# Windowed attention and a gated feed-forward block in one kernel: where the first gate's and the first value's products stand on TensorE

## The chip, the cores and the metric

The kernel runs on one core of a Trainium2 chip. The metric is the device time of one execution in microseconds (us), lower is better.

## What is computed

Attention over 8 batches, 8 heads, 576 positions and 64 features a head, with a causal window of 64 positions, followed by a gated feed-forward block over the 4608 tokens (512 features, 1536 hidden). Cut to what matters:

```python
scores = scale * np.matmul(q, k.transpose(0, 1, 3, 2))
mask = (rel >= 0) & (rel < 64)          # rel = query position - key position
scores = np.where(mask, scores, -1e9)
attn = softmax(scores)
x = np.matmul(attn, v)                  # heads side by side: (4608, 512)
gate = 1.0 / (1.0 + np.exp(-(x @ w_gate)))
val = x @ w_val
out = (gate * val) @ w_out
```

The three weights arrive as float64 and are turned into float32 on the chip.

## The kernel before, in words

Tokens are worked on in 12 tiles of 384. Attention is cut into units: a unit (t, p) is tile t and one pair of heads p, p from 0 to 3. The program has three stages. The front computes the attention of tiles 0 and 1, eight units in a row. The second stage runs the feed-forward block of tiles 0 and 1 with plain products, while the weights are still being converted and tile 2 and 3's attention is slipped in. The rest takes two tiles at a time with seven combined products in place of eight, and the next tiles' attention between them.

A unit of the front passes through all engines:

- `scores` (line 220, tile `s`): 24 small matmuls on TensorE, into two banks of the accumulation memory (PSUM), one for each half h.
- `exponentials`: VectorE adds the mask, scales and takes the row minimum (line 244, tiles `p` and `mn`), three instructions a half; ScalarE takes the exponentials (line 252), three a half. For the first half it also sums them.
- `normalize`: VectorE sums the second half (line 265), corrects and inverts the sums (lines 259 and 260, tile `rs`), GpSimd multiplies (line 269).
- `stage_b`: TensorE transposes the two halves (line 301, tile `pp`), ScalarE copies them out (line 306, tile `pT`).
- `stage_c`: 24 small matmuls give the unit's attention output (line 331, tile `oo`). `x_split` turns it into a high part, which ScalarE rounds off (line 338), and a low part, which VectorE gets by subtraction (line 339): tile `x`.

In the feed-forward block `up` (line 362, tile `ph`) makes one 128 x 384 piece of the hidden layer with 12 matmuls: for each of the four head pairs high weight times high x, high weight times low x, low weight times high x. `up_gate` does this with the gate's weight and takes the sigmoid on ScalarE (line 371, tile `g`). `up_val` does it with the value's weight and multiplies by the gate on VectorE (line 395). `down` adds the piece to the outputs (line 409, tile `y`). The weights are converted by ScalarE (lines 117 and 118), VectorE (lines 126 to 130), ScalarE again (line 158) and VectorE (line 159), each kind shortly before its use, with DMAs of the converted weights to memory (line 154) in the queue of SyncE.

What sets the order: every step is put into a list with a time and a rank, the list is sorted by both, and the steps are written in that order. TensorE keeps the written order (`keep_in_program_order`). The other engines are ordered by a scheduler, with one rule that matters here: exponentials and sigmoids need different function tables in ScalarE, so all of them form one chain in written order (`table_order`, with `chain`), and a table load stands wherever the chain goes from one kind to the other. All engines execute their instructions in order.

The times of the front are written out by hand. Unit n (0 to 7) has its scores at -40 + 3.6n and its softmax 3.5 later. So the softmax of unit (1,2), n = 6, has the time -14.9 (in floating point -14.899999999999999), the scores of unit (1,3) have -14.8 and its softmax has -11.3. The first gate, `up_gate` of tile 0 and piece 0, is at -9.9 and the first value at -7.8.

The banks for the `ph` tiles go round among three; the first gate's was last used by the scores of unit (1,1).

Of the kernel before, what the change touches and what calls it, by code (L numbers as in the profile page):

```python
# [26 lines left out]
def attn_ffn(ctx: ExitStack, tc: tile.TileContext, qT, kT, vN, w_gate, w_val, w_out, out, outT):  # L27
# [57 lines left out]
    def pe(ins):  # L85
        return tc.keep_in_program_order(ins)
# [262 lines left out]
    def h_bank(nm):  # L349
        nbank[0] += 1  # L350
        return psum(0, nbank[0] % 3, nm)[:, :TT]

    def up(t, j, m):
        ph = h_bank(f"ph{m}_{t}_{j}")
        w2 = wgv[m][j]
        prs = []
        for p in range(NP):
            whi, wlo = (w2[:, p // 2, e, p % 2 * P:(p % 2 + 1) * P] for e in range(2))
            xh, xl = xs[(t, p)][:, 0, :], xs[(t, p)][:, 1, :]
            prs += [(whi, xh), (whi, xl), (wlo, xh)]  # L360
        for i, (l, r) in enumerate(prs):
            pe(nc.tensor.matmul(ph, l, r, start=i == 0, stop=i == len(prs) - 1))  # L362
        return ph
# [12 lines left out]
    def up_gate(t, j):  # L376
        gate_table(t, j, up(t, j, 0))
# [13 lines left out]
    def up_val(t, j):  # L391
        ph = up(t, j, 1)
        g = gates.pop((t, j))
        h32 = mp.tile([P, TT], F32, name=f"h32_{t}_{j}", tag="c", bufs=CB)
        nc.vector.tensor_mul(out=h32, in0=ph, in1=g)
        last = hidden_split(t, j, h32, nc.vector)
        if t == 0:
            marks[j] = (chain[-1], last.ins)
# [103 lines left out]
    def sums_make(m, k):  # L502

        a1, a2 = sums[m, k]
        sw = mp.tile([P, 4, H], F32, name=f"sw_{m}_{k}", tag="raw", bufs=RAW)
        lo, up = ([slice(h + c, h + c + P) for c in range(0, H, P)] for h in (0, H))
        for c, d in zip(lo, up):
            nc.gpsimd.tensor_add(out=sw[:, 0, c], in0=a2[:, c], in1=a2[:, d])
        for c in lo:
            nc.gpsimd.tensor_sub(out=sw[:, 1, c], in0=sw[:, 0, c], in1=a1[:, c])  # L510
        for c in lo:
            nc.gpsimd.tensor_sub(out=sw[:, 2, c], in0=a1[:, c], in1=a2[:, c])
        for c, d in zip(lo, up):
            nc.gpsimd.tensor_sub(out=sw[:, 3, c], in0=a1[:, d], in1=sw[:, 1, c])
        sums[m, k] = sw
# [189 lines left out]
    UPT, DNT, PRT = 4.2, 2.1, 1.05  # L705
    events = []

    def put(tm, o, f, *a):
        events.append((tm, o, f, a))
# [16 lines left out]
    for n in range(2 * NP):  # L726
        t, p = divmod(n, NP)
# [17 lines left out]
    at, now = {}, 0.0  # L745
# [5 lines left out]
    def attend(i):  # L751
        nonlocal now
        for f, t, p, *done in fill.get(i, ()):
            if f in (0, 3):
                put(now - LOAD_AHEAD, 8, load_qk, t, p)
                put(now - LOAD_AHEAD, 8.5, load_v, t, p)
            put(now, 6, stages[f], t, p, *done)
            now += APT[f]

    for i, (kind, t, j) in enumerate(plan):  # L760
        attend(i)
        at[(kind, t, j)] = now
        if (kind, t, j) == ("up", 0, 0):
            now = -9.9
        if kind == "up":
            put(now, 9, up_gate, t, j)
            now += UPT / 2
            attend(i + 0.5)
            put(now, 9, up_val, t, j)
            now += UPT / 2  # L770
        else:
            for x in range(TB):
                put(now + x * DPT, 9, down, t, j, x, j == 0, j == NF - 1)
            now += DNT
        if (kind, t, j) == ("up", 0, 0):
            now = 0.0
    for i in range(KINDS * NF):
        j, m = divmod(i, KINDS)
# [125 lines left out]
    for tm, _, f, a in events:  # L904
        if f in (conv_a, conv_b, conv_c):
            with ExitStack() as behind:
# [4 lines left out]
                j, m = divmod(a[0], KINDS)  # L911
# [56 lines left out]
```

## Time and profile before

| | |
|---|---|
| median of 3 runs | 961.45 us (961.2 to 963.39) |
| profiled execution | 961.67 us, of which the span from first to last instruction is 959.9 us |
| TensorE busy | 941.3 us (98%) |
| TensorE weight loads busy | 898.0 us (94%) |
| VectorE, ScalarE, GpSimd busy | 714.3, 602.7, 147.5 us |
| granted TensorE clock, mean over the span | 0.998 |

PE is TensorE, PEld its weight loads, DVE is VectorE, ACT ScalarE, POOL GpSimd, SP SyncE. Rows of the timeline give the start in us from the span's start, the length, engine, line, operation, output<-input, size, the number of merged instructions, and in brackets the idle time before the row with what ended it. Rows of the windows give, for each stretch, its length and the busy time of every engine, the granted TensorE clock as a fraction of full speed (PEclk), the DMA share and the GB/s.

### The profile page before, as it was taken

Reading aid. Unit: us, or ns where it says so; the run is one execution under the profiler, and the core shown is the slowest. Engines: PE = TensorE matmul, PEld = TensorE weight load, DVE = VectorE, ACT = ScalarE, POOL = GpSimd, SP = SyncE. Lnnn points to the kernel's source line nnn. Section 1 sums busy time; section 2 is a strip of 40 time slices with the busy share of each in tenths; the row PEclk is TensorE's granted clock in tenths of the full one; section 3 lists DMA queues with packets and bytes.
Section 4 is the critical chain, followed back from the end, with each engine's and each line's share of the span. In section 5 each row is a group of like instructions: output and inputs, shape, how many; then the busy total and the mean of one; then the engine's idle time right before and its main releaser. Section 6 shows DMA issues by size and latency. Waiting matters only on the chain.

```text
span 959.9 us, 20420 instructions
## 1 busy us (share of the span) xinstructions
PE 941.3 (98%) x7164; PEld 898.0 (94%) x7164; DVE 714.3 (74%) x1919; ACT 602.7 (63%) x1487; POOL 147.5 (15%) x232
## 2 busy tenths in 40 slices
PE   6899999999999999999999999999999999999998
PEld 5799998879998999999999999999999999999998
DVE  7898989788778985666976576796566697567782
ACT  7878878667677754766755666764666675222350
POOL 4210103703765000110100111100110100000000
PEclk9999999999999999999999999999999999999999
DMA  9899988979988999888889888879988868988464
GB/s 339 304 357 370 347 303 271 347 275 358 369 301 271 402 325 309 277 265 269 251 260 316 267 273 261 270 256 284 302 273 249 268 220 257 314 249 251 143 217 157
DMA packets 105510, 273.45 MB, mean 285 GB/s; under 512 B 11456, under 2 KB 33600, under 8 KB 105408
## 3 DMA queue, kind: packets, MB, share of 16 engines
q1 hardware_dynamic: 105408, 272.15, 84.7%
q8 instruction: 57, 0.93, 0.4%
q14 instruction: 45, 0.37, 0.1%
HBM read 220.20 MB, written 51.90 MB: 283 GB/s over the span
## 4 chain that ended last, share of the span: by engine, by line
PE 77%; ACT 6%; DVE 5%; DMA 5%; issue 3%; POOL 2%; SPq 0%; DVEq 0%; ACTq 0%; POOLq 0%
PE pr L586 42%; PE y L586 23%; PE s L220 3%; PE pp L301 2%; PE ph L362 2%; PE y L409 2%; DMA w32d<-w 2%; PE s L331 2%; ACT p L252 2%; DMA a<-w32d 1%; PE oo L331 1%; DVE w L130 1%; POOL ws L528 1%; ACT L252 1%; ACT raw L118 1%
## 5 line engine op out<-in xcount | busy, mean ns | idle before, releaser
L586 PE MATMUL pr<-x_T,wt 128*128 128x384 f32 x1224 | 227.5, 338 | 0.0
L586 PE MATMUL y<-h,wot 128*128 128x384 f32 x1260 | 219.9, 334 | 0.0
L586 PEld LDWEIGHTS y<-h,wot 128*128 128x128 f32 x1260 | 218.2, 188 | 0.6 <-DVE h L629 0.3
L586 PEld LDWEIGHTS pr<-x_T,wt 128*128 128x128 f32 x1224 | 211.6, 188 | 4.5 <-issue 3.6
L586 PE MATMUL pr<-x_B,wt 128*128 128x384 f32 x1008 | 189.4, 336 | 0.0
L586 PEld LDWEIGHTS pr<-x_B,wt 128*128 128x128 f32 x1008 | 174.7, 188 | 0.8 <-issue 0.5
L668 ACT CAST h<-h 128x384 fp32r<-128x384 f32 x210 | 102.7, 515 | 80.6 <-PE y L586 43.3
L269 POOL TENSOR_TENSOR p<-p,rs 128x384 f32<-128x384 f32 x76 | 66.4, 890 | 551.8 <-DVE rs L260 496.7
L669 DVE TENSOR_TENSOR h<-h,h 128x384 fp32r<-128x384 f32 x210 | 110.7, 554 | 26.8 <-ACT h L668 26.1
L252 ACT ACTIVATE p<-p,mn 128x128 f32<-128x128 f32 x288 | 110.9, 393 | 10.2 <-DVE mn L244 9.7
L362 PE MATMUL ph<-x,w 128*128 128x384 f32 x576 | 107.0, 339 | 1.3 <-ACT g L371 0.8
L362 PEld LDWEIGHTS ph<-x,w 128*128 128x128 f32 x576 | 99.5, 188 | 4.3 <-ACT g L371 1.4
L371 ACT ACTIVATE g<-c 128x384 f32<-128x384 f32 x90 | 46.6, 524 | 66.3 <-DVE c L625 65.9
L244 DVE CUSTOM_DVE_ANT_0 p<-s,m 128x128 f32<-128x128 f32 x288 | 65.3, 284 | 27.6 <-PE s L220 27.5
L629 DVE TENSOR_TENSOR h<-c,g 128x384 f32<-128x384 f32 x90 | 55.5, 616 | 30.2 <-ACT g L371 24.7
L371 ACT ACT_TABLE_LOAD x40 | 51.3, 1283 | 12.7 <-DVE c L625 11.4
L220 PE MATMUL s<-k,q 64*64 64x128 f32 x1152 | 46.5, 293 | 7.2 <-DMA k<-in_kT_dram 5.8
L596 DVE TENSOR_TENSOR c<-pr,p 128x384 f32<-128x384 f32 x60 | 33.0, 550 | 23.7 <-PE pr L586 23.7
L252 ACT ACT_TABLE_LOAD x39 | 50.0, 1283 | 0.7
L252 ACT ACTIVATION_READ_ACCUMULATOR p<-p,mn 128x1 f32 x264 | 49.8, 188 | 0.0
L220 PEld LDWEIGHTS s<-k,q 64*64 64x64 f32 x1152 | 34.2, 141 | 13.9 <-DMA q<-in_qT_dram 5.2
L301 PE MATMUL pp<-ident,p 128*128 128x128 f32 x288 | 42.6, 281 | 4.6 <-POOL p L269 2.6
(106 smaller groups left out, 1215.9 us busy)
## 6 DMA issues: line engine op xcount, KB each, us to landing
wt<-wd SPq DMA_DIRECT2D x186, 512.0 KB, 4.5
wot<-wod SPq DMA_DIRECT2D x105, 512.0 KB, 4.7
v<-in_vN_dram SPq DMA_DIRECT2D x48, 384.0 KB, 5.4
wd<-ws SPq DMA_DIRECT2D x48, 256.0 KB, 4.4
k<-in_kT_dram SPq DMA_DIRECT2D x48, 224.0 KB, 5.2
q<-in_qT_dram SPq DMA_DIRECT2D x48, 192.0 KB, 5.1
w32d<-w SPq DMA_DIRECT2D x36, 256.0 KB, 4.6
wd<-w SPq DMA_DIRECT2D x36, 256.0 KB, 5.8
```

The costliest lines, as they stand in the source:

```text
L220: pe(nc.tensor.matmul(sc[h][half * BLK:(half + 1) * BLK, u, :], qt[h * BLK:(h + 1) * BLK, U * BLK:(U + 1) * BLK], kt[h * BLK:(h + 1) * BLK ...
L244: nc.vector.tensor_tensor_reduce(out=pt[:, u, :], in0=sc[:, u, :], in1=masks[key], op0=ALU.add, op1=ALU.min, scale=-SCALE, scalar=3.0e38, ...
L252: exp = nc.scalar.activation(pt[:, u, :], pt[:, u, :], AF.Exp, bias=mn[:, u:u + 1], scale=-1.0, **sums)
L269: eng.tensor_mul(out=pt, in0=pt, in1=rs.unsqueeze(2).broadcast_to([P, UP, P]))
L301: pe(nc.tensor.transpose(pp[:, u, :], pt[:, u, :], ident))
L362: pe(nc.tensor.matmul(ph, l, r, start=i == 0, stop=i == len(prs) - 1))
L371: act = nc.scalar.activation(g, c, AF.Sigmoid)
L586: pe(nc.tensor.matmul(ps, l, r, start=first and i == 0, stop=last and i == 2, skip_group_check=not check))
L596: marks["plus"] = nc.vector.tensor_add(out=o, in0=ps, in1=a).ins
L629: nc.vector.tensor_mul(out=hidden(s, k)[2 * r + b], in0=c, in1=gates.pop((t, j)))
L668: nc.scalar.copy(h2[:, 0, :], src)
L669: nc.vector.tensor_sub(out=h2[:, 1, :], in0=src, in1=h2[:, 0, :].bitcast(F32))
```

## The change

The first gate's time becomes -14.9, and the first value's -9.9, the time that the gate had. In `up`, the first gate alone (tile 0, piece 0; the value too, since both go through the same function) takes the matmul with the low part of the last head pair's x at the very end of its twelve.

```diff
@@ up
             prs += [(whi, xh), (whi, xl), (wlo, xh)]
+        if t == 0 and j == 0:
+            prs.append(prs.pop(-2))
         for i, (l, r) in enumerate(prs):
@@ the plan
         if (kind, t, j) == ("up", 0, 0):
-            now = -9.9
+            now = -9.9 - UPT / 2
         if kind == "up":
-            put(now, 9, up_gate, t, j)
+            put(now if t + j else -14.9, 9, up_gate, t, j)
             now += UPT / 2
             attend(i + 0.5)
             put(now, 9, up_val, t, j)
```

`UPT / 2` is 2.1. Lines behind the change are two higher in the changed kernel (362 becomes 364, 371 becomes 373).

On TensorE, from the transposes of unit (1,0) to the outputs of unit (1,2), the order before is this (`s0_1_3` is the first half of unit (1,3)'s scores, `pp1_1_0` the second half of unit (1,0)'s transposes, `ph0_0_0` the first gate's piece, `ph1_0_0` the first value's; rows of the same kind are left out):

```order
L301 MATMUL pp1_1_0_652<-ident_105,p1_1_0_525 128x128 x3
L220 MATMUL s0_1_3_682<-k_3_227,q_1_3_253 64x128
...
L301 MATMUL pp1_1_1_718<-ident_105,p1_1_1_598 128x128 x3
L362 MATMUL ph0_0_0_748<-x_0_0_420,w0_0_479 128x384 x3
...
L331 MATMUL oo_1_1_763<-pT0_1_1_716,v_1_1_248 64x64
...
L301 MATMUL pp1_1_3_797<-ident_105,p1_1_3_736 128x128 x3
L362 MATMUL ph1_0_0_803<-x_0_0_420,w1_0_624 128x384 x3
...
L331 MATMUL oo_1_2_822<-pT0_1_2_783,v_1_2_256 64x64
```

The first gate's twelve stand between the transposes and the outputs of unit (1,1), the first value's twelve between the transposes of units (1,2) and (1,3) and the outputs of unit (1,2). And the same stretch of TensorE in the changed kernel:

```order
L301 MATMUL pp1_1_0_652<-ident_105,p1_1_0_525 128x128 x3
L364 MATMUL ph0_0_0_658<-x_0_0_420,w0_0_479 128x384 x3
...
L220 MATMUL s0_1_3_697<-k_3_227,q_1_3_253 64x128
...
L301 MATMUL pp1_1_1_733<-ident_105,p1_1_1_598 128x128 x3
L364 MATMUL ph1_0_0_763<-x_0_0_420,w1_0_624 128x384 x3
...
L331 MATMUL oo_1_1_782<-pT0_1_1_731,v_1_1_248 64x64
...
L301 MATMUL pp1_1_3_816<-ident_105,p1_1_3_751 128x128 x3
L331 MATMUL oo_1_2_822<-pT0_1_2_802,v_1_2_256 64x64
```

The gate's twelve now stand ahead of unit (1,3)'s scores, the value's twelve have the gate's old place, and nothing stands between the transposes of unit (1,3) and the outputs of unit (1,2).

On ScalarE, in the same part of the program, the order before is this (`p0_1_2` and `p1_1_2` are the exponentials of unit (1,2)'s halves, `g_0_0` is the first gate's sigmoid):

```order
L306 COPY pT1_1_0_656<-pp1_1_0_652 128x384
L252 ACTIVATE p0_1_2_658,rs_1_2_660<-p0_1_2_658,mn0_1_2_659 128x128 x3
L252 ACTIVATE p1_1_2_670<-p1_1_2_670,mn1_1_2_671 128x128 x3
L252 ACTIVATE p0_1_3_724,rs_1_3_726<-p0_1_3_724,mn0_1_3_725 128x128 x3
L252 ACTIVATE p1_1_3_736<-p1_1_3_736,mn1_1_3_737 128x128 x3
L338 CAST x_1_0_709<-oo_1_0_696 128x384
L306 COPY pT0_1_1_716<-pp0_1_1_712 128x384
L306 COPY pT1_1_1_722<-pp1_1_1_718 128x384
L371 ACT_TABLE_LOAD
L371 ACTIVATE g_0_0_761<-ph0_0_0_748 128x384
```

All exponentials of the front, then the copies of unit (1,1), then one table load and the sigmoid. The same part of ScalarE in the changed kernel:

```order
L306 COPY pT1_1_0_656<-pp1_1_0_652 128x384
L373 ACT_TABLE_LOAD
L373 ACTIVATE g_0_0_671<-ph0_0_0_658 128x384
L252 ACT_TABLE_LOAD
L252 ACTIVATE p0_1_2_673,rs_1_2_675<-p0_1_2_673,mn0_1_2_674 128x128 x3
L252 ACTIVATE p1_1_2_685<-p1_1_2_685,mn1_1_2_686 128x128 x3
L252 ACTIVATE p0_1_3_739,rs_1_3_741<-p0_1_3_739,mn0_1_3_740 128x128 x3
L252 ACTIVATE p1_1_3_751<-p1_1_3_751,mn1_1_3_752 128x128
L338 CAST x_1_0_724<-oo_1_0_711 128x384
L252 ACTIVATE p1_1_3_751<-p1_1_3_751,mn1_1_3_752 128x128 x2
L306 COPY pT0_1_1_731<-pp0_1_1_727 128x384
L306 COPY pT1_1_1_737<-pp1_1_1_733 128x384
```

Since -14.9 sorts just ahead of -14.899999999999999, the first gate is written before the softmax of unit (1,2). The sigmoid with its table load, and a load of the exponentials' table, now stand ahead of the exponentials of units (1,2) and (1,3). A third load stands later, before the next sigmoid, that of tile 1. VectorE has the sums of unit (1,2) (line 259) now between the mask steps of unit (1,3)'s two halves instead of ahead of them.

## The prediction

> **What bounds the kernel now.** I read the windows first, to see where TensorE idles, then the timelines of TensorE, ScalarE and VectorE around the change. The windows of the span:
>
> ```profile
> 42.00:100.00 58.00, 58.00 (x420) 54.09 (x416) 52.42 (x140) 48.14 (x107) 4.85 (x5) 1.00 1.01 359
> 100.00:200.00 100.00, 97.54 (x728) 86.64 (x727) 87.62 (x223) 77.09 (x172) 31.23 (x48) 1.00 0.87 301
> 200.00:300.00 100.00, 97.85 (x792) 90.61 (x791) 79.06 (x227) 69.69 (x178) 52.33 (x100) 1.00 0.96 339
> 300.00:940.00 640.00, 640.00 (x4689) 624.84 (x4688) 461.87 (x1167) 373.13 (x923) 42.64 (x52) 1.00 0.83 270
> ```
>
> After the stretch length comes TensorE's busy time. From 42 us to 100 us it never idles, from 300 to 940 neither, and between 100 and 300 it idles 2.46 + 2.15 = 4.6 us. So whatever moves the start of tile 1's first gate, at 42.16 us, moves the end by as much, less what those 4.6 us take back. The change lies ahead of that point. TensorE there:
>
> ```profile
> 23.56 0.89 PE L220 MATMUL s<-k,q 64*64 64x128 f32 x24
> 25.04 1.29 PE L331 MATMUL oo<-pT,v 128*64 128x64 f32 x24 [0.59 <-ACT pT L306]
> 26.26 0.55 PE L301 MATMUL pp<-ident,p 128*128 128x128 f32 x3
> 27.37 0.55 PE L301 MATMUL pp<-ident,p 128*128 128x128 f32 x3 [0.56 <-POOL p L269]
> 28.72 0.40 PE L220 MATMUL s<-k,q 64*64 64x128 f32 x2 [0.79 <-PE pp L301]
> 29.47 1.55 PE L220 MATMUL s<-k,q 64*64 64x128 f32 x22 [0.35 <-DVE rs L260]
> 30.95 1.55 PE L331 MATMUL oo<-pT,v 128*64 128x64 f32 x24
> 32.42 0.90 PE L301 MATMUL pp<-ident,p 128*128 128x128 f32 x6
> 33.08 2.35 PE L362 MATMUL ph<-x,w 128*128 128x384 f32 x12
> 35.36 0.92 PE L331 MATMUL oo<-pT,v 128*64 128x64 f32 x24
> ...
> 42.16 8.62 PE L362 MATMUL ph<-x,w 128*128 128x384 f32 x48
> ```
>
> The scores of unit (1,3), 28.72 us, come after an idle 0.79 us and are broken by another 0.35: their two banks are still being read by the mask steps of unit (1,2). That is the 1.14 us which the first gate's products now fill. The rows behind it are slow: 22 scores take 1.55 us where 24 took 0.89 at 23.56, and 24 output matmuls 1.55 where 24 take 0.92 at 35.36. The granted clock says why:
>
> ```profile
> 29.00:29.50 0.50, 0.15 (x6) 0.07 (x5) 0.50 (x6) 0.50 (x4) 0.00 (x0) 0.59 1.03 403
> 32.50:33.00 0.50, 0.50 (x5) 0.50 (x6) 0.35 (x5) 0.50 (x4) 0.17 (x1) 0.99 1.10 430
> ```
>
> The third figure from the end is the clock. It is at half from about 29.09 us (0.59 over 29.0 to 29.5) to about 32.51 us (0.99 over 32.5 to 33.0), 3.4 us long, which costs about 1.7 us of work. In the 3.4 us ahead of that, 25.68 to 29.09, TensorE was busy 1.13 + 0.55 + 0.37 = 2.05 us by the rows above, 60%.
>
> **The change on TensorE.** No matmul is added or taken away. The gate's twelve can start when the transposes of unit (1,0) end, at 27.37 + 0.55 = 27.9 us. Their bank is long free, their weight long converted. The last x they need is the low part of unit (0,3), the second row here:
>
> ```profile
> 29.03 0.28 DVE L244 CUSTOM_DVE_ANT_0 p<-s,m 128x128 f32<-128x128 f32 x1
> ...
> 29.33 0.53 DVE L339 TENSOR_TENSOR x<-oo,x 128x384 fp32r<-128x384 f32 x1
> ```
>
> It lands at 29.86. Eleven of the twelve matmuls take 11/12 of the 2.35 us in the row at 33.08, so the moved twelfth is due at about 30.05 and waits for nothing, and the gate ends at 27.9 + 2.35 = 30.25 us. The banks for the scores are free by 29.3 (the first row: the last mask step of unit (1,2)), so the scores follow without a gap, at full clock. Up to here the change gains.
>
> **The change on ScalarE.** Here it loses. ScalarE's rows of before:
>
> ```profile
> 27.65 0.86 ACT L306 COPY pT<-pp 128x384 f32<-128x384 f32 x2
> 28.39 0.42 ACT L252 ACTIVATE p<-p,mn 128x128 f32<-128x128 f32 x1
> ...
> 29.55 0.98 ACT L252 ACTIVATE p<-p,mn 128x128 f32<-128x128 f32 x3
> 31.48 0.40 ACT L252 ACTIVATE p<-p,mn 128x128 f32<-128x128 f32 x1 [0.94 <-DVE mn L244]
> ...
> 33.53 0.45 ACT L338 CAST x<-oo 128x384 fp32r<-128x384 f32 x1
> 33.89 0.84 ACT L306 COPY pT<-pp 128x384 f32<-128x384 f32 x2
> 35.51 1.28 ACT L371 ACT_TABLE_LOAD   x1 [0.77 <-PE ph L362]
> 36.80 0.49 ACT L371 ACTIVATE g<-ph 128x384 f32<-128x384 f32 x1
> 37.19 0.47 ACT L338 CAST x<-oo 128x384 fp32r<-128x384 f32 x1
> ...
> 38.68 1.23 ACT L306 COPY pT<-pp 128x384 f32<-128x384 f32 x3
> ```
>
> By the order, the load for the sigmoid now follows the copies of 27.65, and the exponentials of unit (1,2), at 28.39 before, are queued behind it. The load waits for the gate: before, its wait ended at 35.51, 0.08 us after the products' end (33.08 + 2.35 = 35.43). So it starts at 30.3; then 1.28 for the load, 0.49 for the sigmoid, 1.28 for the load back: the exponentials start at 33.4 instead of 28.4, 5.0 us later. Between 28.39 and 33.89 there were 5.50 us, of which 0.94 idle, in which the exponentials of unit (1,3) waited for the mask steps. That idle goes, since the scores are done by 31.1 and the mask steps of the first half by about 31.8. Those of the second half now stand on VectorE behind the sums of unit (1,2), which wait until 33.4 + 1.16 = 34.6; with three steps of some 0.21 they end at 35.4, and ScalarE wants them at about 36.6: no cost. So the copies of unit (1,1) start at 33.4 + 4.56 = 38.0 and end at 38.8, against 34.73 before.
>
> The price of a change of table is open to doubt. These rows show a load between two other instructions:
>
> ```profile
> 58.54 0.60 ACT L158 CAST w<-w 128x512 fp32r<-128x512 f32 x1
> 59.16 1.28 ACT L252 ACT_TABLE_LOAD   x1
> 60.46 0.40 ACT L252 ACTIVATE p<-p,mn 128x128 f32<-128x128 f32 x1
> ```
>
> From the cast's end at 59.14 to the exponential at 60.46 are 1.32 us, so I keep 1.28 and a few hundredths. [...]
>
> **Back on TensorE.** After the gate come scores, outputs of unit (1,0), transposes of (1,1) and the value's products: 0.89 + 0.92 + 0.90 + 2.35, a little less for their overlaps, so TensorE is through at about 35.0. The outputs of unit (1,1), in order the next, need both copies: 38.8. That is a new idle stretch of 3.8 us in place of the old 1.14. From there the path goes through both engines:
> - outputs of (1,1): 1.55 us at half clock, 0.92 at full. By a stretch that was 60% busy the clock fell, so I take half: to 40.25.
> - ScalarE then has the cast of that output and a weight's conversion ahead of the copies of unit (1,2): 38.68 - 37.19 = 1.49 us, and two copies 0.86: 42.65. Before, the value's products hid this stretch; now nothing does.
> - outputs of (1,2) and (1,3), about 1.5 us each at half clock: 45.65. The third and fourth copy are done in time.
>
> So tile 1's gate starts at 45.65 instead of 42.16, 3.5 us later. At full clock all along it would be 43.9, 1.7 us later.
>
> To this comes what is left of the half clock once TensorE is busy again. It came back at 32.51 after 3.4 us of which TensorE was idle for the 0.35 us above; counted from 42.65, that leaves 0 to 3.4 us of half clock behind 45.65, a cost of 0 to 1.7; I take 0.7, a little under the middle, since the transposes already keep TensorE busy before. The 4.6 us of later idle take something back, 0 to 1; I take 0.4, since the engines that make TensorE wait there are late by about as much. Sum: 3.5 + 0.7 - 0.4 = 3.8 us on the profiled execution's 961.67, so 965.5. The median of the runs shown is 0.2 below that execution: **965.3 us**.
>
> In SyncE's queue two loads of tile 2's v move ahead of a weight's load and a store. The stores of converted weights (line 154) follow the late conversions by some 3 us, as TensorE does. I give neither a price of its own: TensorE needs no v of tile 2 before many more products, and what the late stores could cost is rival D.
>
> **The rivals.** Each time is on the scale of the profiled execution.
>
> - B, the clock holds: the new 3.8 us of idle are not enough to halve it, and the delay is 1.7 us, of which 0.4 are taken back later: 963.0, within 0.3% of before (about what a measurement can tell, 2.9 us), so not slower by that bound. It decides whether the outputs of unit (1,1) run at 0.9 or 1.55 us. Against it: the clock halved at 29.09 after gaps of 0.56 and 0.79 us in 3.4 us. [...] Chance 0.20.
> - C, the gain comes through: ScalarE's lateness is hidden, the 1.14 us gap and the 1.7 us of half clock are saved: 958.8, faster. It would need the copies of (1,1) by 35.0, so a sigmoid that costs the exponentials less than 1.2 us in place of 5.0. The chain in written order leaves no room for that. Chance 0.04.
> - D, the conversions become late as well: a third load, 1.28 us, stands before tile 1's sigmoid, and behind it the next value's weight:
>
> ```profile
> 45.85 0.61 ACT L158 CAST w<-w 128x512 fp32r<-128x512 f32 x1
> ...
> 47.31 0.68 DVE L159 TENSOR_TENSOR w<-w,w 128x512 fp32r<-128x512 f32 x1
> ```
>
>   It is done at 47.99, and its products start three quarters into the 8.62 us row, at 48.6: 0.6 us to spare, so 0.7 short if both engines are equally late, here and once more at the next weight: 966.9. For it: ScalarE has no idle around there. Against: TensorE at half clock gives that time back. Chance 0.11.
> - E, a change of table costs more than its load row. The nearest row for that is the idle 0.77 us ahead of the load at 35.51, if it were not the wait for the matmuls that it is: twice on the path, 967.0. Against it are the 1.32 us between cast and exponential. [...] Chance 0.02.
>
> **How the numbers follow.** The forecast has the remaining 0.63, with a range of its own from 964.2 to 966.8. Slower by over 0.3%, above 964.3: 0.59 of the forecast, D and E, 0.72. Within: B and the low edge of the forecast, 0.24. Faster: C, 0.04. The range reaches down to B with half a microsecond of its own doubt, and up to D: 962.5 to 967.4; C, E and the edges, under 0.2, stay out.
>
> **What would show it.** In the changed kernel's profile: the gate's twelve at about 27.9 with no gap before the scores; a table load on ScalarE that waits for them until 30.3, and a second one before the exponentials at 33.4; TensorE idle from about 35 to 38.8 before the outputs of unit (1,1), ended by the copies `pT`; half clock behind it; tile 1's gate at 45 to 46. It would be wrong if the exponentials of unit (1,2) began before 30, if that idle were under 1.5 us, or if the clock stayed at full through 36 to 46.

## The result, and the profile after

| | before | changed |
|---|---|---|
| median, 13 runs each | 962.05 us (960.33 to 963.4) | 964.18 us (963.71 to 965.86) |
| ratio | | 1.0028, 95% interval 1.0019 to 1.0037 |
| profiled execution | 961.67 us, span 959.9 | 964.2 us, span 962.4 |

Slower by 0.28%, with an interval that lies on both sides of the 0.3% line. Ratios, here and below, are recorded from the fast executions alone, without one of before at 1027.49 us and one of a later kernel at 3349.57 us, and are not quite the quotient of the two medians, which here is 1.0022. Forecast was 965.3. On the profiled executions the change costs 2.5 us, where the sum said 3.8. TensorE's timeline of the changed kernel, in the columns of the prediction:

```profile
27.58 2.67 PE L364 MATMUL ph<-x,w 128*128 128x384 f32 x12
30.18 0.89 PE L220 MATMUL s<-k,q 64*64 64x128 f32 x24
31.00 0.92 PE L331 MATMUL oo<-pT,v 128*64 128x64 f32 x24
31.85 0.87 PE L301 MATMUL pp<-ident,p 128*128 128x128 f32 x6
32.48 2.35 PE L364 MATMUL ph<-x,w 128*128 128x384 f32 x12
38.39 1.92 PE L331 MATMUL oo<-pT,v 128*64 128x64 f32 x24 [3.56 <-ACT pT L306]
40.24 2.82 PE L301 MATMUL pp<-ident,p 128*128 128x128 f32 x12
42.99 1.93 PE L331 MATMUL oo<-pT,v 128*64 128x64 f32 x48
44.85 8.59 PE L364 MATMUL ph<-x,w 128*128 128x384 f32 x48
```

Two rows say the most. The gate's twelve run at 27.58 and the scores follow without a gap, so the old 1.14 us are gone. And ahead of the outputs of unit (1,1), at 38.39, stand 3.56 us of idle that the copies `pT` end. Why those copies are late is in ScalarE's timeline:

```profile
27.55 0.87 ACT L306 COPY pT<-pp 128x384 f32<-128x384 f32 x2
30.34 1.28 ACT L373 ACT_TABLE_LOAD   x1 [1.92 <-PE ph L364]
31.63 0.49 ACT L373 ACTIVATE g<-ph 128x384 f32<-128x384 f32 x1
32.14 1.28 ACT L252 ACT_TABLE_LOAD   x1
33.43 0.40 ACT L252 ACTIVATE p<-p,mn 128x128 f32<-128x128 f32 x1
...
37.88 0.83 ACT L306 COPY pT<-pp 128x384 f32<-128x384 f32 x2
```

ScalarE waits 1.92 us for the gate's products, then loads, takes the sigmoid, loads back, and only at 33.43 comes to the exponentials that it began at 28.39 before. Windows of the changed kernel, the length, the busy time of each engine, the clock, the DMA share and the GB/s:

```profile
33.48:36.89 3.41, 1.35 (x8) 1.03 (x6) 2.09 (x12) 3.41 (x16) 0.83 (x1) 1.00 0.93 347
36.89:40.30 3.41, 1.91 (x25) 1.71 (x25) 2.77 (x9) 1.82 (x6) 2.24 (x3) 0.50 0.09 35
40.30:43.71 3.41, 3.41 (x27) 3.08 (x28) 2.37 (x4) 3.31 (x8) 0.40 (x1) 0.50 0.00 0
...
42.00:100.00 58.00, 58.00 (x452) 53.84 (x452) 52.07 (x134) 50.38 (x107) 4.35 (x4) 0.99 0.96 343
100.00:200.00 100.00, 97.28 (x710) 87.08 (x709) 86.42 (x224) 77.02 (x177) 31.37 (x48) 1.00 0.90 313
200.00:300.00 100.00, 97.75 (x790) 90.29 (x789) 79.43 (x219) 70.48 (x179) 50.90 (x98) 1.00 0.94 334
```

The clock is at half from 36.89 to 43.71, two stretches of 3.41 us, twice as long as before. Tile 1's gate starts at 44.85 instead of 42.16, 2.69 us later. TensorE's idle time from 100 to 300 us is 2.72 + 2.25 = 4.97 us against 4.61, so nothing of the delay is taken back there.

### The profile page after: what moved, and what is told of

Its sections match the earlier page's. It is cut to its first block, busy times and chain, and to the rows that moved or that the text cites. A ratio compares the mean times of both kernels' runs of the same rounds, so it can differ in the third digit from the quotient of the medians.

```text
span 962.4 us, 20416 instructions
## 1 busy us (share of the span) xinstructions
PE 939.9 (98%) x7164; PEld 897.1 (93%) x7164; DVE 714.1 (74%) x1919; ACT 606.3 (63%) x1489; POOL 147.3 (15%) x232
## 4 chain that ended last, share of the span: by engine, by line
PE 82%; DMA 7%; ACT 5%; DVE 2%; issue 2%; POOL 1%; SPq 1%; DVEq 0%; POOLq 0%; ACTq 0%
PE pr L588 41%; PE y L588 23%; PE ph L364 7%; PE s L220 3%; PE pp L301 3%; PE y L411 2%; DMA a<-w32d 2%; PE s L331 2%; ACT p L252 2%; PE oo L331 1%; DMA v<-in_vN_dram 1%; DMA q<-in_qT_dram 1%; DMA wd<-ws 1%; DMA k<-in_kT_dram 1%; ACT L252 1%
## 5 line engine op out<-in xcount | busy, mean ns | idle before, releaser
L306 ACT COPY pT<-pp 128x384 f32<-128x384 f32 x96 | 41.3, 479 | 11.0 <-PE pp L301 10.8
```

Source lines behind the costliest of these rows:

```text
L306: cp = nc.scalar.copy(pT, pp)
```

## The experiments

Twelve kernels, in four groups, each group timed beside the kernel before on one chip (medians of before: 961.72, 961.49, 961.85 and 961.94). Ratios are to before, with their 95% interval.

### Is it the sigmoid with its loads, or the products?

**sig_mid** moves the sigmoid and its two loads from ahead of the exponentials of (1,2) to behind them.

```diff
-            put(now if t + j else -14.9, 9, up_gate, t, j)
+            put(now if t + j else -14.85, 9, up_gate, t, j)
```

> The changed kernel with the first gate at -14.85 instead of -14.9, so written behind the softmax of unit (1,2) and still ahead of unit (1,3)'s scores: on ScalarE the two loads and the sigmoid stand between the exponentials of (1,2) and of (1,3). Theory S: the exponentials of (1,3) start at 33.6, the copies of (1,1) end at 36.9 instead of 38.7, tile 1's gate at 42.0 to 43.0, time 962.0 to 962.8, half to all of the change's loss gone. Theory V: no difference from the change, tile 1's gate at 44.9, 964.2.

Measured: 961.68 us, ratio 0.9998 (0.9988 to 1.0007), 0.3 us under theory S's range: the whole loss is gone. Its ScalarE, and its TensorE:

```profile
29.48 0.99 ACT L252 ACTIVATE p<-p,mn 128x128 f32<-128x128 f32 x3
30.48 1.28 ACT L373 ACT_TABLE_LOAD   x1
```

```profile
36.51 1.58 PE L331 MATMUL oo<-pT,v 128*64 128x64 f32 x24 [1.68 <-ACT pT L306]
38.02 2.82 PE L301 MATMUL pp<-ident,p 128*128 128x128 f32 x12
40.77 1.62 PE L331 MATMUL oo<-pT,v 128*64 128x64 f32 x48
42.32 8.59 PE L364 MATMUL ph<-x,w 128*128 128x384 f32 x48
```

The first load follows the exponentials of (1,2) with no wait, since the gate's products are done by then. The idle falls from 3.56 to 1.68 us and tile 1's gate starts at 42.32. A step of 0.05 in a number took the whole loss away.

**no_load** takes an exponential in the place of the first gate's sigmoid, which it leaves out; the products stay where the change put them.

```diff
-            act = nc.scalar.activation(g, c, AF.Sigmoid)
+            act = nc.scalar.activation(g, c, AF.Sigmoid if t + j else AF.Exp)
```

> The changed kernel with an exponential in place of the first gate's sigmoid (its output is wrong there), so that ScalarE waits for the gate's products in the same place but loads no table before or behind it. Theory S: exponentials of (1,2) at 30.8 instead of 33.4, copies of (1,1) done at 36.1, tile 1's gate 2.6 us earlier than in the change, at 42.2, or up to 0.7 better where the clock holds; 961.0 to 962.0. Rival W (the wait for the products, not the loads, sets the delay): tile 1's gate at 44 or later, 963.5 or more. Theory V: 963 or more.

Measured: 960.77 us, 0.9992 (0.9983 to 1.0). ScalarE:

```profile
30.40 0.49 ACT L373 ACTIVATE g<-ph 128x384 f32<-128x384 f32 x1 [1.93 <-PE ph L364]
30.79 0.39 ACT L252 ACTIVATE p<-p,mn 128x128 f32<-128x128 f32 x1
```

The wait for the products is the same 1.93 us, and ScalarE still handles the gate first. Only the two loads are missing, and tile 1's gate starts at 41.11, against 42.16 before and 44.85 with the change; theory S had 41.5 at best, and 961.0. So it is the loads that decide, not the wait.

**sig_late** keeps the products at -14.9 and writes the sigmoid at -9.95.

```diff
-            put(now if t + j else -14.9, 9, up_gate, t, j)
+            if t + j:
+                put(now, 9, up_gate, t, j)
+            else:
+                put(-14.9, 9, gate_products)
+                put(-9.95, 9, gate_sigmoid)
```

> The changed kernel with the first gate's sigmoid written at the gate's old time, so behind all exponentials of the front; the gate's and the value's products stand where the change puts them. Theory S (the change loses because the sigmoid and two table loads stand ahead of the exponentials of units (1,2) and (1,3), and the move of the products itself gains): exponentials of (1,2) at 28.3 as before, copies of (1,1) done by 34.7, no idle before the outputs of (1,1), tile 1's gate at 40 to 41 instead of 42.2, time 960.2 to 961.0, about 1.5 us under the kernel before. Theory V (the loss is the value's products, which no longer hide the stretch before the outputs of unit (1,2)): tile 1's gate at 43 or later and a time of 963 or more.

Measured: 962.96 us, 1.0012 (1.0001 to 1.0024), so not the gain that an earlier start should bring: tile 1's gate starts where theory S has it, but the time is 2 us over its range, close to theory V's. TensorE:

```profile
39.00 2.06 PE L331 MATMUL oo<-pT,v 128*64 128x64 f32 x48 [1.28 <-ACT pT L306]
40.98 1.56 PE L364 MATMUL ph<-x,w 128*128 128x384 f32 x7
42.92 7.38 PE L364 MATMUL ph<-x,w 128*128 128x384 f32 x41 [0.38 <-DVE x L339]
```

Tile 1's gate starts 1.18 us ahead of before, waits 0.38 for the residual of unit (1,3), and TensorE idles 5.87 us from 42 to 300, against 4.61.

**val_old** has the products early, the sigmoid at -9.9 and the value in its old place.

```diff
-            now = -9.9 - UPT / 2
+            now = -9.9
...
+                put(-14.9, 9, gate_products)
+                put(-9.9, 9, gate_sigmoid)
```

> The first gate's products early as in the change, its sigmoid behind all exponentials, and the value's products back in their old place between the transposes of (1,3) and the outputs of (1,2). Theory S: TensorE waits about 1.9 us for the copies of (1,1), done at 34.7, and the value's products hide the later wait: tile 1's gate at 40.5 to 41.3, 960.4 to 961.2, about as good as with the value early. Theory V: clearly better than with the value early, by 1.5 us or more.

Measured: 964.8 us, 1.0029 (1.0019 to 1.0039), as slow as the change itself, which neither theory had, by another wait. TensorE, then ScalarE:

```profile
42.56 0.91 PE L331 MATMUL oo<-pT,v 128*64 128x64 f32 x22 [1.74 <-ACT pT L306]
```

```profile
40.13 0.62 ACT L158 CAST w<-w 128x512 fp32r<-128x512 f32 x1 [0.34 <-DVE w L130]
42.03 0.48 ACT L306 COPY pT<-pp 128x384 f32<-128x384 f32 x1 [1.28 <-DVE h L405]
```

The last copy of unit (1,3) stands behind a weight's cast and waits for its buffer, the tile `g` that the first value's multiplication still reads. That multiplication is late here. Gate early and value late was never a cheap half of the change.

### Is it the clock, and is an early start worth anything?

**warm** is the changed kernel with 18 more matmuls into the value's bank ahead of the real twelve, which start the bank anew.

```diff
+        if t == 0 and j == 0 and m == 1:
+            for n in range(18):
+                l, r = prs[n % 12]
+                pe(nc.tensor.matmul(ph, l, r, start=n == 0, stop=n == 17))
```

> The changed kernel with 18 more matmuls of the first value's products ahead of its twelve, into the same bank, which the real twelve then overwrite: some 3.2 us of work in the idle stretch before the outputs of unit (1,1), so that the clock holds. Theory H (the half clock behind the idle stretch costs about a microsecond): idle before the outputs of (1,1) under 0.7 us, clock at full from 27 to 46, outputs of (1,1) in 1.3 us instead of 1.92, transposes then bound by GpSimd's last product at 40.7, tile 1's gate at 43.4 to 44.0 instead of 44.85, time 962.8 to 963.4. Rival: the clock costs nothing there, since ScalarE and GpSimd set the pace: tile 1's gate at 44.8, 964.2.

Measured: 963.97 us, 1.0026 (1.0014 to 1.0037). TensorE:

```profile
38.40 1.29 PE L331 MATMUL oo<-pT,v 128*64 128x64 f32 x24 [0.48 <-ACT pT L306]
...
43.77 8.72 PE L368 MATMUL ph<-x,w 128*128 128x384 f32 x48
```

The clock stays at full, 1.00 in every half microsecond from 26 to 50 us, and tile 1's gate starts 1.08 us earlier than in the change, but no gain can be measured. TensorE now idles 0.82 us from 42 to 100, where the change has none; from 100 to 300 it idles 4.08 against 4.97, and the span is still only 0.2 us shorter. So the half clock of the change, two stretches here, costs its front about 1.1 us, but to take it away with added matmuls gains nothing that shows.

**val_only** leaves the gate where it was and puts the value directly behind it.

```diff
-            now = -9.9
+            now = -9.9 - UPT / 2
...
-            put(now, 9, up_gate, t, j)
+            put(now if t + j else -9.95, 9, up_gate, t, j)
```

> The kernel before with the first value's products directly behind the first gate's, both ahead of the outputs of unit (1,1); the gate stays in its old place. Alone this takes away the cover of the wait for unit (1,2)'s copies. Theory S: outputs of (1,1) at 37.5 instead of 35.4, ScalarE's casts and copies behind them later by as much less 0.9, tile 1's gate at 42.5 to 43.1, time 0.3 to 0.9 us over before, 962.0 to 962.6. Theory V (the value's cover is what the change loses): 963.5 or more.

Measured: 961.91 us, 1.0009 (1.0 to 1.0019). Tile 1's gate starts at 41.11, as in no_load and earlier than either theory had it, but TensorE idles 6.80 us from 42 to 300, and nothing is won. How much of the early start is due to the value's move stays open: in the execution shown the half clock lay at 21.33 to 24.75 us and not at 29.09 to 32.51 as before, so the gate's twelve, ahead of the value, already began at 31.75 instead of 33.08.

**cast_behind** is sig_late with the cast of the third conversion behind the copies of unit (1,3).

```diff
-        put(tm + (2.5 if i > 1 else 3.5), 2, conv_c, i)
+        put(tm + (5 if i == 3 else 2.5 if i > 1 else 3.5), 2, conv_c, i)
...
+                if a[0] == 3 and f is conv_c:
+                    behind.enter_context(tc.issue_after(marks["1_3"][0]))
```

> The kernel with the late sigmoid, and the cast of the next gate's weight (line 158, third weight conversion) put behind the casts of the last two units' outputs on ScalarE, where it stood ahead of them and waited 0.96 us for VectorE. Theory F (what took the late-sigmoid kernel's gain is the wait at the end of the front, x casts queued behind a cast that waits for VectorE): x casts at 39.9 and 41.0 instead of 41.6 and 41.9, tile 1's gate runs through without the 0.38 us wait, first down products (line 409) at 49.2 to 49.6 instead of 50.15, time 0.5 to 0.9 us under the late-sigmoid kernel, about 962.2. Rival G (the conversions of the weights and their DMAs set the pace up to 100 us, so TensorE only waits elsewhere): down products may come earlier, but the time stays at 962.9 and waits for the gate or for products behind 50 us grow by as much.

Measured: 964.52 us, 1.0035 (1.0023 to 1.0048), slower than either theory has it. Tile 1's gate starts at 40.97 with no wait, the best front of all, and the kernel has the highest median of this group. TensorE, and an earlier row of ScalarE:

```profile
61.03 2.00 PE L364 MATMUL ph<-x,w 128*128 128x384 f32 x10 [1.59 <-DVE w L159]
```

```profile
52.49 0.66 ACT L117 ACTIVATE w<-raw 128x512 f32<-128x512 f32 x1 [3.52 <-DMA w32d<-w]
```

TensorE runs into a weight that isn't converted yet. The conversions themselves wait: ScalarE stands 3.52 us until a store of a converted weight (line 154) is through, where the kernel before stands 1.46 us at the same line. The wait for the weight is less than half of the idle time that this kernel adds behind the front (table below); the rest falls on other waits.

**exp_cast** adds to that the first sigmoid as an exponential, an addition and a reciprocal on VectorE.

```diff
-            act = nc.scalar.activation(g, c, AF.Sigmoid)
+            if t + j:
+                act = nc.scalar.activation(g, c, AF.Sigmoid)
+            else:
+                act = nc.scalar.activation(g, c, AF.Exp, scale=-1.0)
+                nc.vector.tensor_scalar_add(g, g, 1.0)
+                nc.vector.reciprocal(out=g, in_=g)
```

> As the kernel with the cast behind, and the first gate's sigmoid made from an exponential: ScalarE takes exp(-x) with the table it has, VectorE adds one and inverts. The table load moves from ahead of unit (1,1)'s cast to the sigmoid of tile 1. If ScalarE's path sets tile 1's gate: cast of (1,1) at 35.9 instead of 37.0, copies of (1,2) 1.1 us earlier, tile 1's gate at 39.9 to 40.4, time 960.8 to 961.5, under the kernel before. If the conversions set the pace (rival G): tile 1's gate earlier, but the time at 962 or more. VectorE's inverse of 128 x 384 has no row yet; if it takes over 2 us, the gain is gone as well.

Measured: 964.11 us, 1.0032 (1.0021 to 1.0044). Tile 1's gate starts at 41.03, later than the 39.9 to 40.4 hoped for. The reciprocal alone holds VectorE 2.55 us, and a weight is waited for twice, 1.7 us in all. In both kernels a conversion is late; in this one the reciprocal stands on the engine that converts, so how much of it is due to that was not separated.

### Does SyncE's queue pace the stretch behind the front?

Across some of these kernels the time seemed to follow the moment at which SyncE issues the first load of raw weights after the front (before 40.67 us, changed 44.69, cast_behind 43.22), since the queue's head waits for the third conversion and the DMA engines have little to do meanwhile (a share of 0.42, 0.13 and 0.17 from 36 to 44 us). Three kernels move that conversion ahead in before, in the changed kernel and in sig_late, with one edit:

```diff
+        if i == 3:
+            tm -= 7
...
-                early = {3: ("1_1",), 2: ("1_3",), 4: ("1_3",), 5: ("1_3",)}.get(a[0], (key,))
+                early = {3: ("0_3",), 2: ("1_3",), 4: ("1_3",), 5: ("1_3",)}.get(a[0], (key,))
```

> The kernel before, with one edit: the third conversion of weights (i = 3) is written 7 slots earlier and may start once the front's unit 0_3 is through, so that ScalarE's two reads of its raw tile stand ahead of the copies of (1,0) at about 27.6 us, and its cast between the exponentials of (1,2) and of (1,3). Theory R (when SyncE's queue gets going again after the front is what the stretch from 42 to 100 us is paced by): the first load of raw after the front, at 40.67 us before, is issued at 31 to 34 us; the DMA share from 36 to 44 us rises from 0.42 to over 0.6; TensorE is not idle from 42 to 100 us; median 960 to 961.3 although tile 1's gate may start up to 1.2 us later than 42.16 (the two reads, 1.24 us, stand ahead of the exponentials of (1,2)). Theory T (only TensorE's start at the front's end counts): the same start of the queue, but the time follows tile 1's gate: 962 to 963 if it starts at 42.8 to 43.4.

> The changed kernel with the same edit for the conversion i = 3; here its cast stands ahead of the table load of the first gate. Theory R: the queue goes on by 31 to 34 us instead of 44.69, the DMA share from 36 to 44 us rises from 0.13 to over 0.5, and most of the change's loss is gone: 961.5 to 963, although tile 1's gate starts no earlier than 44.85 (up to 46.5, since 1.24 us of reads and a cast of 0.62 us stand ahead of the exponentials). Theory T: 964.5 to 966, with tile 1's gate at 45 to 46.5.

> The version with the gate's products early and its sigmoid late, with the same edit for the conversion i = 3. Theory R: the queue goes on by 31 to 34 us instead of 42.55, and the early start of TensorE is at last worth something: 959.5 to 961, under the kernel before, with no wait of tile 1's gate on the residual sums and TensorE's idle time from 42 to 100 us at 0 to 0.5 us instead of 1.23. Theory T: the 1.24 us ahead of the exponentials delay tile 1's gate from 40.98 to 42 or later and nothing is won: 962 to 963.

Measured: before_c7 963.62 us, 1.0017 (1.0003 to 1.0031); after_c7 967.52, 1.006 (1.0041 to 1.0078); sig_late_c7 963.47, 1.0015 (1.0003 to 1.0027). SyncE's queue and a window of before_c7:

```profile
33.36 0.96 SPq L105 DMA_DIRECT2D raw<-in_moe_w_gate_dram  x1
```

```profile
36.00:44.00 8.00, 7.70 (x103) 7.04 (x102) 3.71 (x10) 5.47 (x12) 1.82 (x3) 1.00 0.66 231
```

The queue went on 7.3 us sooner and the DMA share from 36 to 44 us rose from 0.42 to 0.66, as planned, and none of the three is faster for it: before_c7 and after_c7 are slower than without the edit, sig_late_c7 (1.0015) can't be told from sig_late (1.0012). Theory R falls. All three also lie above theory T's ranges, by 0.5 to 1.5 us, and for before_c7 and sig_late_c7 not by its mechanism alone, since they start tile 1's gate at 42.71 and 42.42 and idle more later (next table). In after_c7 ScalarE's order is to blame at once:

```profile
32.34 0.62 ACT L158 CAST w<-w 128x512 fp32r<-128x512 f32 x1 [2.62 <-DVE w L130]
```

The cast stands ahead of the table load and waits 2.62 us for VectorE, so everything the change made late is later still: TensorE idles 6.03 us before the outputs of (1,1).

### Taking the loads away and keeping the sigmoid

**tanh_gate** works out the first gate's sigmoid from a tanh.

```diff
-            act = nc.scalar.activation(g, c, AF.Sigmoid)
+            if t + j:
+                act = nc.scalar.activation(g, c, AF.Sigmoid)
+            else:
+                act = nc.scalar.activation(g, c, AF.Tanh, scale=0.5)
+                nc.vector.tensor_scalar(out=g, in0=g, scalar1=1.0, scalar2=0.5, op0=ALU.add, op1=ALU.mult)
```

> The changed kernel, with the first gate's sigmoid worked out as 0.5 * (1 + tanh(x / 2)): a tanh on ScalarE, for which the built program needs no other table than the exponentials', and one operation of VectorE on 128x384, 0.36 us by the row of an addition on such a tile in the run with the exponential as a sigmoid, at about 30.9 us, where VectorE was idle in the run with an exponential in the sigmoid's place (1.47 us before 31.27). Theory S (the loss is the two table loads and the sigmoid ahead of the exponentials of (1,2)): no table load from 27 to 41 us, exponentials of (1,2) from 30.8 us, one half-clock window at most, tile 1's gate at 41 to 41.5 us, median 960.3 to 961.5, 3 us under the changed kernel and level with the kernel before or up to 1 us under it. Rival (the cost is the wait for the gate's products, whatever the function): tile 1's gate at 43 us or later, 962.5 to 964.5.

Measured: 960.36 us, 0.9986 (0.9977 to 0.9995), the one kernel whose interval lies wholly under the kernel before; with 0.14% it is less than the 0.3% that counted as no change here. ScalarE, VectorE, TensorE and the windows:

```profile
30.44 0.49 ACT L376 ACTIVATE g<-ph 128x384 f32<-128x384 f32 x1 [1.93 <-PE ph L364]
30.82 0.39 ACT L252 ACTIVATE p<-p,mn 128x128 f32<-128x128 f32 x1
```

```profile
30.96 0.36 DVE L377 TENSOR_SCALAR g<-g 128x384 f32<-128x384 f32 x1 [1.11 <-ACT g L376]
31.31 0.29 DVE L244 CUSTOM_DVE_ANT_0 p<-s,m 128x128 f32<-128x128 f32 x1
```

```profile
35.77 1.29 PE L331 MATMUL oo<-pT,v 128*64 128x64 f32 x24 [0.88 <-ACT pT L306]
...
41.13 8.59 PE L364 MATMUL ph<-x,w 128*128 128x384 f32 x48
```

```profile
42.00:100.00 58.00, 58.00 (x414) 53.74 (x412) 52.87 (x141) 50.68 (x108) 6.34 (x6) 1.00 1.01 363
100.00:200.00 100.00, 97.11 (x726) 86.54 (x725) 86.51 (x223) 76.44 (x173) 30.91 (x48) 1.00 0.88 300
200.00:300.00 100.00, 98.34 (x797) 91.14 (x796) 80.47 (x228) 70.54 (x183) 52.44 (x100) 1.00 0.95 340
```

No table load stands between tanh and exponentials (starts at 30.44 and 30.82), VectorE's extra 0.36 us lie in a gap, the idle before the outputs of (1,1) is 0.88 us, and the start at 41.13 is kept: 2.89 + 1.66 = 4.55 us of idle from 100 to 300, none before.

## Where an early start goes

From 300 to 940 us TensorE never idles, in any of these kernels. So the end is set by when TensorE gets through the front and by how long it idles from there to 300. I take the first row of `y` in the second stage as the front's end, 50.62 us before, and TensorE's idle time from there to 300, 4.61 us before. Differences to before, from one profiled execution each:

| kernel | first `y` | idle from there to 300 | sum | span |
|---|---|---|---|---|
| changed | +2.66 | +0.36 | +3.0 | +2.5 |
| warm | +1.71 | +0.24 | +2.0 | +2.3 |
| val_old | +1.23 | +0.84 | +2.1 | +1.6 |
| sig_mid | +0.13 | +0.37 | +0.5 | +0.1 |
| no_load | -1.06 | +0.64 | -0.4 | -0.7 |
| tanh_gate | -1.06 | -0.06 | -1.1 | -1.3 |
| val_only | -1.06 | +2.19 | +1.1 | +1.6 |
| sig_late | -0.47 | +0.89 | +0.4 | +0.5 |
| cast_behind | -1.22 | +3.52 | +2.3 | +3.8 |
| exp_cast | -0.14 | +2.21 | +2.1 | +3.2 |
| before_c7 | +0.52 | +1.90 | +2.4 | +3.0 |
| sig_late_c7 | +0.23 | +2.07 | +2.3 | +3.0 |
| after_c7 | +4.74 | +0.12 | +4.9 | +4.8 |

The two columns account for the span to about 1 us, for cast_behind to 1.5. The rest is TensorE's busy time behind the first `y`, which for the same 6661 matmuls is 900.99 us before and 902.50 in cast_behind. The three that are latest at the front (after_c7, changed, warm) idle hardly more later; before_c7 and sig_late_c7, a little late, idle some 2 us more. Of the six that are early, four idle more by more than they had won. In which order ScalarE and VectorE do conversions, exponentials and copies behind 42 us differs in each, since their scheduler places them anew, and the waits fall on different things: a sigmoid (2.2 us in sig_late), a weight, a product of GpSimd (1.4 us in before_c7). val_only and tanh_gate have the same front and differ by 2.25 us of idle. No single cause of that was found, and it stays open. Nor do the rows carry more than one execution can: in the one of before the half clock fell on TensorE's work at 29.09 to 32.51 us, so up to about 1.3 us of what the first column shows as gained can be the clock's (an estimate from the start of the gate's twelve, 33.08 before and 31.75 in val_only), and executions of one kernel often lie 2 us apart (val_only's here is 1.35 us over its median, val_old's 1.5 us under).

## Why the prediction was right, and where not

- **TensorE's gain**: the gate was put at 27.9 to 30.25; it ran from 27.58 to 30.25. Right.
- **ScalarE's loss**: load at 30.3, exponentials at 33.4, copies from 38.0 to 38.8; measured 30.34, 33.43, and 37.88 to 38.71. From the first load's start to the first exponential are 3.09 us, the three rows' 1.28 + 0.49 + 1.28 and 0.04 between them. So here a table change cost its row and a few hundredths, and rival E isn't there. That the loads are the cause was shown by sig_mid, no_load and tanh_gate.
- **The idle**: 3.8 forecast, 3.56 measured; the outputs of (1,1) began at 38.39, on the first of the two copies, where the prediction had them need both. They ended at 40.31, forecast 40.25, at half clock as forecast. Rival B, the clock that holds, did not happen, though the time came out about midway between its 963.0 and the forecast's 965.5. Nor was it the luck of one execution: the mean clock was 0.997 or less in 10 of the 13 of the changed kernel and 0.998 in the others, while of 88 of the kernel before 18 had 0.997 or less and 21 had 1.000.
- **Outputs of (1,2) and (1,3)**: "copies done at 42.65, then about 1.5 us each at half clock". They began at 42.99, not on the copies: the transposes before them took 2.82 us at half clock and ended at 43.06. I had left them out as done in time. They then took 1.93 us together, not 3.0, since the clock was back at 43.71.
- **The leftover half clock, 0.7** is the term that failed, with the one before it: "counted from 42.65, that leaves 0 to 3.4 us". TensorE was busy again from 38.39, when the outputs of (1,1) start. From 40.30 to 43.71 it was busy throughout, 3.41 us of transposes and small matmuls at half clock, and the clock was back at full at 43.71, before tile 1's gate began at 44.85. Leftover: 0.
- **Taken back later, 0.4**: 0.2 by the spans, 2.69 at the start of tile 1's gate and 2.5 at the end. It did not come from the idle, which grew by 0.36, but from the busy time behind the first `y`, 0.5 shorter.
- **The sum**: 2.69 + 0 - 0.2 = 2.5 for 3.5 + 0.7 - 0.4 = 3.8. Two steps of its path are added up wrongly (38.8 + 1.55 is 40.35, and 40.25 + 1.49 + 0.86 is 42.60), but the slips nearly cancel. The range held the time. Of the chances, the likeliest, slower by over 0.3%, is missed by the point value and touched by the interval.
- **A premise that fails for early starts**: "whatever moves the start of tile 1's first gate moves the end by as much". For the three latest fronts (changed, warm, after_c7) it does, to within 0.7 us. For an early start it mostly does not, as the table shows, and before_c7, 0.55 us late there, ends 3.0 us late. TensorE's idle of 0.00 from 42 to 100 us hid that VectorE at 52.4 of 58 us and the DMA share at 1.01 were nearly as full. Had the change come without its loads, my gain for it (rival C, 958.8) would have been too large: tanh_gate took 960.36.

## What to carry to other kernels

When products move, look at what else rides on them in the written order: here a sigmoid brought two table loads of 1.28 us into a chain of exponentials, and a function with no load ahead of it or behind it (an exponential, a tanh), or a place 0.05 later in the list, undid the loss. A stretch in which one engine never idles need not pass on an earlier start; before counting a gain through it, look at how full the others are, and at whether their order stays what it was.

## What the runs showed of the hardware

In seven of the fourteen profiled executions the clock falls once between 16 and 50 us, and each time it stays at half for 3.41 us or twice that. Of the time ahead of 16 us I make nothing: the recorded clock says 1.00 there, while 24 scores of before take 1.56 us at 4.00 and at 11.54 in place of 0.89 at 15.74. In the 3.41 us just ahead of the fall TensorE was busy 0.32 us (after_c7), 1.35 (changed), 1.68 (sig_mid), 1.78 (val_only), 1.79 (tanh_gate), 1.80 (before_c7) and 2.05 (before, 60%). Where the half clock lasted twice as long, TensorE was busy 0.48 us (after_c7) and 1.91 (changed) in the first 3.41 us of it; in the last 3.41 us before the clock came back it was busy from 3.07 us (before) to 3.42 (after_c7). The busy time alone does not decide: in changed it was 2.00 us from 16.41 to 19.82, and in sig_late_c7, where TensorE idles 2.61 us ahead of 37.48, 0.85 us from 34.5 to 38.0, and in both the clock was at full during that and for the 3.41 us behind it. What else decides was not shown. One stretch of 3.41 us after which the clock fell, and two after which it held:

```profile
17.92:21.33 3.41, 1.78 (x30) 1.18 (x29) 3.38 (x20) 3.41 (x10) 1.57 (x2) 1.00 1.06 386
```

```profile
16.41:19.82 3.41, 2.00 (x30) 1.39 (x28) 3.34 (x16) 3.41 (x13) 2.10 (x2) 1.00 1.05 388
```

```profile
27.99:31.41 3.42, 2.27 (x51) 1.81 (x51) 3.39 (x18) 3.42 (x13) 1.47 (x2) 1.00 1.04 402
```

They are from val_only, changed and before_c7. The place of the half clock changes from run to run. val_only has the same instructions as before up to the gate, but its half-speed stretch is from 21.33 to 24.75 us and that of before from 29.09 to 32.51, so the 1.7 us which I had read as a cost of the scores' place belong to no instruction.

What a stretch is worth in the time of the kernel before can be read from its executions. One stretch of 3.41 us at half makes a mean clock of 0.998 over 960 us (3.41 / 2 / 960 is 0.0018). Of the 88 executions beside the twelve kernels, the 21 at 1.000 took 961.05 us on average, the 54 at 0.997 to 0.999 took 961.97, and the 13 at 0.996 took 962.30.
